# A convolution and SwiGLU kernel: block 0 convolved on TensorE by doubled diagonals, weights cast by GpSimd transfers, another order in the last block

## The chip, the core and the metric

The kernel runs on one NeuronCore of a Trainium2 chip. The metric is device time in microseconds (us), as the median of several executions. One more execution was taken by the hardware profiler; all durations below are from it, and "the profile" and "the trace" mean it. Engine names: PE is TensorE, DVE is VectorE, ACT is ScalarE, POOL is GpSimd, SP is SyncE (here only a DMA queue). An instruction named L320 stands on line 320 of the kernel as it is before the change.

## The reference

```python
w = softmax(weight, axis=-1)              # 8 heads x 7 taps
x_pad = zeros(6 rows) ++ x                # x: 8 x 4096 x 192, causal
conv[b, s, h, :] = sum_k w[h, k] * x_pad[b, s + k, h, :]    # 24 channels a head
y = conv.reshape(32768, 192)
out = (silu(y @ w_gate) * (y @ w_val)) @ w_out              # 192 -> 1536 -> 192
```

A depthwise convolution of seven taps, shared by the 24 channels of a head, feeds a gated feed-forward layer over 32768 tokens. Input and output are float32; the kernel multiplies in float16 and accumulates in float32.

## The kernel before, in words

**Tiling.** Tokens are taken in 64 blocks of 512 (TB). Two blocks are a pair. 192 channels are 128 + 64, so a pair of blocks is laid out as three groups of 128 partitions: group 0 holds channels 0 to 127 of the pair's first block, group 1 the last 64 channels of the first block and the first 64 of the second, group 2 the rest of the second block. Each group is convolved as one tile of 128 x 512 (xc), and a copy with its two halves of 64 partitions exchanged (xs, made by two small transfers on SP, L283 and L284) lets every 64 channels be met from either half of the PE array.

**A block's matmuls.** The 1536 features are 12 chunks of 128. I number the chunks through the run: 0 to 11 are block 0, 12 to 23 block 1, 24 is the first chunk of block 2. For each chunk `first` issues three steps; a step is one matmul for the gate on the lower 64 rows of the array (L313) and one for the value on the upper 64 rows (L314), which run side by side, so that a step takes the time of one. Then `gate` gives ACT a silu (L318) and DVE the product h = silu * val (L320). `second` issues the output matmuls (L325) of the block before, eight to a chunk, into a pair of banks (acc), and after six chunks ACT copies acc out (`evacuate`, L363) and SP stores it (L355). PSUM holds two gate buffers, three value buffers, one buffer for a convolution's running sum (run) and acc, which takes two banks and has one buffer.

**The order around it.** Nothing is scheduled automatically: each engine executes its instructions in the order in which the program issues them. The convolution of a later pair is strewn over the chunks by a plan (PLAN, `at_chunk`, `plan_group`): x is cast into a DRAM copy by a POOL transfer (L80), transposed by a transfer on SP (L85), and for each group, from a chunk c on, ACT makes tap 0 (run, L249) at c and two more taps at c+2 and c+4 (L253), DVE adds two taps at c+1 and c+3 (L260), POOL makes two taps (L267) and adds everything up (L273, L277) from c+4, and SP exchanges the halves at c+11. For pair 1 the three c are 6, 10 and 16. The run buffer is single, so a group's tap 0 waits until DVE has finished the group before it.

**The opening (block 0 and 1 before the plan runs).** x of both blocks is loaded by SP (L105); the softmax of the taps is computed on 8 partitions and spread to all channels by fp32 matmuls (L193, wn_ps). Blocks 0 and 1 are cast by POOL and ACT (L199 to L202), transposed by PE (L228, L230) and convolved as three groups: group 0 by ACT and DVE taps (L249, L253, four DVE taps L260, joined at L277), group 1 on PE by 14 matmuls with diagonal matrices (L390; a weight's float16 part and the rest, seven taps each), group 2 by ACT, DVE and POOL after that, beside block 0's first chunks. Two PE matmuls with a permutation exchange halves (L411). The first four chunks' gate and value weights are staged in float32 by SP (L122) and cast by ACT and POOL (L394, L418); the other weights are cast by POOL's transfers (L127). `warm` issues idle matmuls (L165).

**The end.** After chunk 767, the last block's output matmuls follow in four runs of 12 pairs over four banks (acc, one gate buffer, one value buffer), with two copies and a store after the third and the fourth.

Of the kernel before, what the change touches and what calls it, by code (L numbers as in the profile page):

```python
# [14 lines left out]
    first=(6, 10, 16),  # L15
# [7 lines left out]
def kernel(  # L23
# [68 lines left out]
    def sync_after(ins, earlier, why="one bank, two halves of the array"):  # L92
# [8 lines left out]
    taps = const_pool.tile([H, K], fp32, tag="taps", name="taps")  # L101
    nc.sync.dma_start(out=taps, in_=weight)
    x_sb = xpool.tile([P, 2 * SUBS, D], fp32, tag="x_sb", name="x_sb", bufs=1)
    halves = [
# [4 lines left out]
        for b in range(2)  # L109
    ]  # L110

    C1 = 4 * P
    w = wpool.tile([P, 3, Dff], fp16, tag="w_sb", name="w_sb")
    w_st = wpool.tile([P, 3, C1], fp32, tag="w_st", name="w_st")
# [5 lines left out]
    for rows, src in w_halves:  # L120
        sync_after(
            nc.sync.dma_start(out=w_st[rows, :, :], in_=src[:, :, 0:C1]), halves[0], "x goes first"  # L122
        )

    def load_w(lo, hi, which):
        rows, src = w_halves[which]
        nc.gpsimd.dma_start(out=w[rows, :, lo:hi], in_=src[:, :, lo:hi])  # L127

    ident32 = const_pool.tile([P, P], fp32, tag="ident32", name="ident32")
    make_identity(nc, ident32)  # L130
    ident = const_pool.tile([P, P], fp16, tag="ident", name="ident")
    nc.vector.tensor_copy(ident, ident32)

    swapper = const_pool.tile([P, P], fp16, tag="swapper", name="swapper")
    nc.vector.tensor_copy(swapper[:, 0:DB], ident[:, DB:P])
    nc.vector.tensor_copy(swapper[:, DB:P], ident[:, 0:DB])
# [4 lines left out]

    opening = ctx.enter_context(ExitStack())
    pool0 = opening.enter_context(tc.tile_pool(name="xts0", bufs=1, space=bass.MemoryType.PSUM))


    zeros = const_pool.tile([P, TB], fp16, tag="zeros", name="zeros")
    nc.vector.memset(zeros, 0.0)
    early = {
        n: pool0.tile(shape, dt, tag=n, name=n)
        for n, shape, dt in (  # L150
            ("xt_act", [P, DB + TB], fp16),
            ("wn_ps", [P, 3, K], fp32),
            ("xtB", [P, DB + TB], fp16),
            ("xt", [P, DB + TB], fp16),
            ("sumB", [P, TB], fp32),
            ("swB", [P, TB], fp32),
            ("idle", [P, TB], fp32),
            ("xtC", [P, DB + TB], fp16),
        )
    }  # L160
    idle = early["idle"]

    def warm(n):
        for _ in range(n):
            nc.tensor.matmul(idle, ident, zeros, start=True, stop=True)  # L165


    own = const_pool.tile([H, 2 * D], fp32, tag="own", name="own")
    nc.gpsimd.memset(own, 1.0)
    for m in (own[:, 0:D], own[:, D:]):  # L170
        nc.gpsimd.affine_select(
            out=m, in_=m, pattern=[[1, D]],
            compare_op=ALU.is_ge, fill=0.0, base=0, channel_multiplier=-grp,
        )
        nc.gpsimd.affine_select(
            out=m, in_=m, pattern=[[-1, D]],
            compare_op=ALU.is_ge, fill=0.0, base=grp - 1, channel_multiplier=grp,
        )
    head = {n: const_pool.tile([H, 1], fp32, tag=n, name=n) for n in ("wmax", "wsum", "wrec")}
    soft = const_pool.tile([H, K], fp32, tag="soft", name="soft")  # L180
    warm(4)
    nc.vector.tensor_reduce(head["wmax"], taps, axis=AX.X, op=ALU.max, negate=True)  # L182
    nc.scalar.activation(soft, taps, AF.Exp, bias=head["wmax"])
    nc.scalar.activation(two, one, AF.Silu)
    nc.vector.tensor_reduce(head["wsum"], soft, axis=AX.X, op=ALU.add)
    nc.vector.tensor_scalar(head["wsum"], head["wsum"], scalar1=1e-9, scalar2=None, op0=ALU.add)
    nc.vector.reciprocal(head["wrec"], head["wsum"])
    nc.vector.tensor_scalar(soft, soft, scalar1=head["wrec"], scalar2=None, op0=ALU.mult)

    wn_ps = early["wn_ps"]  # L190
    wn = const_pool.tile([P, 3, K], fp32, tag="wn", name="wn")
    for g in range(3):
        nc.tensor.matmul(wn_ps[:, g, :], own[:, ts(g, P)], soft, start=True, stop=True)  # L193
    warm(2)
    nc.vector.tensor_copy(wn, wn_ps)

    x16 = xpool.tile([P, 1 + SUBS, 2, D], fp16, tag="x16", name="x16", bufs=1)
    nc.gpsimd.memset(x16[:, 0, 0, :], 0.0)
    nc.gpsimd.tensor_copy(x16[:, 1:, 0, 0:P], x_sb[:, 0:SUBS, 0:P])  # L199
    nc.scalar.copy(x16[:, 1:, 0, P:D], x_sb[:, 0:SUBS, P:D])  # L200
    nc.scalar.copy(x16[:, :, 1, 0:DB], x_sb[:, SUBS - 1 :, 0:DB])
    nc.gpsimd.tensor_copy(x16[:, :, 1, DB:D], x_sb[:, SUBS - 1 :, DB:D])  # L202
    for b in range(2):
        load_w(C1, 2 * C1, b)

# [8 lines left out]

    class Group:


        def __init__(self, p, g, pool=cpool):
            self.p, self.g, self.w, self.pool = p, g, wn[:, g, :], pool
            if p:  # L220
                self.xc_in = xts[p][:, g, HIST - pad :]
            self.parts = []

        def rows(self, s):
            return x16[:, s, :, :].rearrange("p b c -> p (b c)")[:, ts(self.g, P)]

        def turn(self, xt, reader=None):
            nc.tensor.transpose(xt[:, 0:DB], self.rows(0)[DB:P, :], ident[DB:P, DB:P])  # L228
            for s in range(SUBS):
                nc.tensor.transpose(xt[:, DB + s * P :][:, 0:P], self.rows(s + 1), ident)  # L230
# [24 lines left out]
        def dve_tap(self, k, psum=False, last=False):  # L255
            v, s = self.tap(k, psum)
            run = self.aD
            if last:
                self.aD = self.pool.tile([P, TB], fp32, tag="aD", name="aD")
# [286 lines left out]
```

## Time and profile before

| what | value |
|---|---|
| median of 3 runs | 780.12 us (780.05, 780.12, 781.20) |
| profiled execution, its own device time | 780.98 us |
| its span from first to last instruction | 779.2 us |
| mean granted PE clock | 0.998 |
| PE busy | 767.4 us, 98% of the span, 10800 matmuls |
| DVE, ACT, POOL busy | 632.8, 661.0, 647.7 us |
| first gate matmul of chunk 0 | 15.47 us |
| first output matmul of block 0 (chunk 12) | 29.03 us |
| last PE matmul begins | 775.5 us |

Start times are counted from the span's start. A timeline row gives start, duration, engine, line, operation, output and input tiles, count, and in brackets how long the engine had idled before and what released it. A busy PE is not a PE at its peak: consecutive matmuls overlap, and what counts is the distance between starts. In the steady part a step of `first` starts every 0.21 us and a pair of output matmuls every 0.08 us.

### The profile page before, as it was taken

The page shows a single profiled execution, that of the slowest core. Times are in us where ns is not written, and L with a number is a line of the kernel's source. Part 1 is how long each engine was busy: PE and PEld are TensorE (multiplying, and loading weights), DVE is VectorE, ACT ScalarE, POOL GpSimd, SP SyncE. Part 2 cuts the span into 40 slices and gives each one's busy share as a digit, 9 for nine tenths or more (in the row PEclk, how much of TensorE's full clock was granted, in tenths as well). Part 3 has the DMA queues.
Part 4 walks back from the last instruction along what each step waited for, and adds up shares of the span by engine and source line. Part 5 has one row for each costly group of instructions (what it writes and reads, how often), then busy time and mean ns, then how long its engine had stood idle before and what let it go on. Part 6 is the DMA issues. An engine that isn't in the chain of part 4 may idle for free.

```text
span 779.2 us, 27410 instructions
## 1 busy us (share of the span) xinstructions
PE 767.4 (98%) x10800; PEld 587.8 (75%) x10800; DVE 632.8 (81%) x980; ACT 661.0 (85%) x1207; POOL 647.7 (83%) x612
## 2 busy tenths in 40 slices
PE   7899999999999999999999999999999999999998
PEld 3567777777777777777777777777777777777776
DVE  6778888888888888888888888888888888888874
ACT  6788888888888888888888888888888888888874
POOL 6799988888888988888988888988888988888820
PEclk9999999999999999999999999999999999999999
DMA  8643553543444454434443435443435443624111
GB/s 154 105 96 67 95 81 89 96 96 68 94 79 93 94 78 86 95 74 98 92 89 77 94 73 99 91 90 77 95 68 102 91 88 81 94 69 103 46 46 53
DMA packets 137186, 67.36 MB, mean 86 GB/s; under 512 B 90080, under 2 KB 136672, under 8 KB 137056
## 3 DMA queue, kind: packets, MB, share of 16 engines
q1 hardware_dynamic: 101440, 51.65, 26.2%
q0 software_dynamic: 35616, 13.95, 16.7%
q8 instruction: 84, 1.38, 0.7%
q14 instruction: 46, 0.38, 0.2%
HBM read 29.47 MB, written 37.74 MB: 86 GB/s over the span
## 4 chain that ended last, share of the span: by engine, by line
PE 97%; ACT 1%; POOL 1%; DMA 0%; DVE 0%; issue 0%; SPq 0%; POOLq 0%; DVEq 0%; ACTq 0%
PE val L314 49%; PE acc L325 34%; PE gate L313 11%; PE sumB L390 1%; ACT silu L318 1%; DMA xs<-xc 0%; PE idle L165 0%; POOL t L273 0%; ACT t L253 0%; DVE h L320 0%; PE wn_ps L193 0%; POOL xc L277 0%; PE gate L325 0%; PE val L325 0%; ACT xc L398 0%
## 5 line engine op out<-in xcount | busy, mean ns | idle before, releaser
L320 DVE TENSOR_TENSOR h<-silu,val 128x512 f16<-128x512 f16 x768 | 512.5, 685 | 133.6 <-ACT silu L318 97.7
L318 ACT ACTIVATE silu<-gate 128x512 f16<-128x512 f32 x768 | 449.3, 593 | 83.2 <-PE gate L313 80.0
L325 PE MATMUL acc<-wo_sb,h 64*128 64x192 f16 x6096 | 474.7, 243 | 0.2 <-DVE h L320 0.2
L325 PEld LDWEIGHTS <-h 64*128 64x128 f16 x6144 | 402.2, 94 | 65.9 <-issue 2.6
L313 PE MATMUL gate<-xs,w_sb 64*128 64x512 f16 x1152 | 428.9, 377 | 1.3 <-ACT silu L318 1.3
L313 PE MATMUL gate<-xc,w_sb 64*128 64x512 f16 x1152 | 428.4, 377 | 1.0 <-ACT silu L318 0.9
L273 POOL TENSOR_TENSOR t<-t,t 128x512 f32<-128x512 f32 x281 | 356.6, 1269 | 85.4 <-ACT t L253 51.6
L314 PE MATMUL val<-xc,w_sb 64*128 64x512 f16 x1152 | 424.0, 377 | 1.1 <-DVE h L320 1.0
L314 PE MATMUL val<-xs,w_sb 64*128 64x512 f16 x1152 | 373.2, 377 | 1.7 <-DMA xs<-xc 1.7
L314 PEld LDWEIGHTS <-w_sb 64*128 64x128 f16 x2304 | 209.4, 94 | 106.9 <-issue 6.0
L313 PEld LDWEIGHTS <-w_sb 64*128 64x128 f16 x2304 | 209.8, 94 | 6.2 <-issue 3.2
L267 POOL TENSOR_SCALAR t<-xt,wn 128x512 f32<-128x512 f16 x186 | 139.0, 828 | 2.2 <-DMA xt<-x16d 2.2
L253 ACT ACTIVATE t<-xt,wn 128x512 f32<-128x512 f16 x186 | 132.6, 713 | 0.0
L277 POOL TENSOR_TENSOR xc<-t,aD 128x512 f16<-128x512 f32 x94 | 119.0, 1266 | 8.0 <-DVE aD L260 0.7
L363 ACT COPY o<-acc 128x384 f32<-128x384 f32 x126 | 60.3, 479 | 20.6 <-PE acc L325 9.1
L260 DVE SCALAR_TENSOR_TENSOR run<-xt,wn,run 128x512 f32<-128x512 f16 x93 | 69.7, 749 | 0.0
L260 DVE SCALAR_TENSOR_TENSOR aD<-xt,wn,run 128x512 f32<-128x512 f16 x93 | 69.0, 742 | 0.0
L249 ACT ACTIVATE run<-xt,wn 128x512 f32<-128x512 f16 x93 | 63.8, 686 | 1.1 <-DVE aD L260 1.1
L80 POOL DMA_DIRECT2D x16d<-in_x_dram x31 | 39.1, 1261 | 0.0
L165 PE MATMUL idle<-zeros,ident 128*128 128x512 f16 x6 | 2.9, 620 | 2.6 <-DVE wmax L182 2.6
L390 PE MATMUL sumB<-xcin,diag 128*128 128x512 f16 x14 | 5.1, 525 | 0.0
L260 DVE SCALAR_TENSOR_TENSOR aD<-xcin,wn,aD 128x512 f32<-128x512 f16 x4 | 3.9, 971 | 0.1
(73 smaller groups left out, 51.3 us busy)
## 6 DMA issues: line engine op xcount, KB each, us to landing
out_dram<-o SPq DMA_DIRECT2D x128, 192.0 KB, 2.2
x16d<-in_x_dram POOLq DMA_DIRECT2D x31, 396.0 KB, 6.1
xs<-xc SPq DMA_DIRECT2D x188, 64.0 KB, 2.8
x_sb<-in_x_dram SPq DMA_DIRECT2D x2, 384.0 KB, 3.6
wo_sb<-in_moe_w_out_dram POOLq DMA_DIRECT2D x1, 576.0 KB, 8.3
xt<-x16d SPq DMA_TRANSPOSE x31, 4.0
w_st<-in_moe_w_gate_dram SPq DMA_DIRECT2D x1, 384.0 KB, 4.4
w_st<-in_moe_w_val_dram SPq DMA_DIRECT2D x1, 384.0 KB, 5.3
```

Source lines behind the costliest of these rows:

```text
L249: nc.scalar.mul(self.aD, *self.tap(0, psum, xt))
L253: nc.scalar.mul(self.parts[-1], *self.tap(k, psum, xt))
L260: nc.vector.scalar_tensor_tensor(out=self.aD, in0=v, scalar=s, in1=run, op0=ALU.mult, op1=ALU.add)
L267: nc.gpsimd.tensor_scalar(self.parts[-1], v, scalar1=s, scalar2=1.0, op0=ALU.mult, op1=ALU.mult)
L273: nc.gpsimd.tensor_tensor(self.parts[0], self.parts[0], t, op=ALU.add)
L277: (eng or nc.gpsimd).tensor_tensor(xc, self.parts[0], self.aD, op=ALU.add)
L313: nc.tensor.matmul(g, w[0:DB, ca, f], a[0:DB, :], start=(i == 0), stop=(i == 2))
L314: nc.tensor.matmul(v, w[DB:P, cb, f], b[DB:P, :], start=(i == 0), stop=(i == 2))
L318: nc.scalar.activation(s, self.g.pop(j), AF.Silu)
L320: nc.vector.tensor_tensor(h, s, self.v.pop(j), op=ALU.mult)
L325: ins = nc.tensor.matmul(acc, self.h[j][r, ts(s, P)], wo_r[r, j, :], start=first and j == 0, stop=not first and j == NCH - 1, skip_group_c ...
L363: nc.scalar.copy(self.o[:, 2 * half : 2 * half + 2, :], self.acc[:, :, 0:D])
```

## The change

Loads: SP loads x first, the taps come on ACT's queue, and all gate and value weights come by six POOL transfers of four chunks and one half of the array each, which cast on the way. The float32 staging tile and its two casts are gone.

Taps: the softmax is no longer divided on 8 partitions. Exponentials and their sum are spread together, and each channel is divided afterwards (`normalize`), first for the two layouts that block 0 needs, and for the two that later groups need at the end of the opening.

Block 0 is convolved wholly on PE. Channels 0 to 127 (A) are multiplied by diagonals that stand doubled, so that each half of 64 channels comes out on both halves of the partitions, in two banks (sum0, sum1), for the float16 part (`hi`) and for the rest (`lo`). The last 64 channels (C) are stored twice, so that one matmul of 128 rows takes both parts (`sum2`). No half of block 0 has to be exchanged any more. Block 1's channels A are convolved by ACT, DVE and POOL taps in the opening, its channels C on PE during chunks 0 to 4 (`lateC`).

Pair 1 of the plan starts at chunks 5, 9 and 16, with three DVE taps and one POOL tap to a group. Chunks 0 and 1 issue their first two steps before either's third.

The end: in the last block the copy out of acc is issued behind the chunk's silu, and the last runs of output matmuls leave chunk 11's pieces for later.

```diff
-    first=(6, 10, 16),
+    first=(5, 9, 16),
...
-    for rows, src in w_halves:
-        sync_after(nc.sync.dma_start(out=w_st[rows, :, :], in_=src[:, :, 0:C1]), halves[0], "x goes first")
+    load_w(0, 4, 0)
+    load_w(0, 4, 1)
...
+            ("xtA", [P, TB], fp16), ("xtC", [P, TB], fp16), ("sum0", [P, TB], fp32),
+            ("sum1", [P, TB], fp32), ("wn_ps", [P, 4, K + 1], fp32), ("sum2", [P, TB], fp32),
+            ("xtA1", [P, DB + TB], fp16),
...
+    def normalize(lo, hi):
+        nc.vector.reciprocal(wrec[:, lo:hi], wn_ps[:, lo:hi, K])
+        nc.vector.tensor_tensor(
+            wn[:, lo:hi, :], wn_ps[:, lo:hi, 0:K],
+            wrec[:, lo:hi].unsqueeze(2).to_broadcast([P, hi - lo, K]), op=ALU.mult,
+        )
+    warm(5)
...
+    spread(0, 2)
+    warm(3)
+    normalize(0, 2)
+    cast_a(nc.gpsimd.tensor_copy, 0, 2)
+    cast_a(nc.scalar.copy, 2, 4)
+    cast_c(nc.vector.tensor_copy, 0, 4)
+    load_w(4, 8, 0)
+    cast_a(nc.gpsimd.tensor_copy, 4, 8)
+    load_w(4, 8, 1)
+    turn(early["xtA"], colA, 0, False)
+    turn(early["xtC"], colC, 0, False)
+    warm(1)
+    nc.vector.tensor_copy(hi, wn[:, 0, :])
+    diagonal(dg["hi"], hi, 0, 4)
+    nc.scalar.copy(xcA[:, pad:], early["xtA"])
+    for k in range(4, K):
+        nc.scalar.mul(dg["hi"][:, k, :], twin, wn[:, 0, k : k + 1])
...
+    diagonal(dg["lo"], lo, 0, K)
+    def conv_a(d, first):
+        for k in range(K):
+            for r, bank in ((slice(0, DB), "sum0"), (slice(DB, P), "sum1")):
+                nc.tensor.matmul(early[bank], d[r, k, :], xcA[r, k : k + TB], ...)
+    def conv_c(bank, xc):
+        for k in range(K):
+            nc.tensor.matmul(bank, dg["C"][:, k, :], xc[:, k : k + TB], ...)
+    conv_a(dg["hi"], True)
+    turn(early["xtA1"], colA, SUBS, True)
+    spread(2, 4)
+    conv_a(dg["lo"], False)
+    for k in range(K):
+        nc.scalar.mul(dg["C"][:, k, :], twin, partC32[:, k : k + 1])
+    nc.scalar.copy(xcC[:, pad:], early["xtC"])
+    conv_c(early["sum2"], xcC)
+    emit_cast(1)
+    cast_c(nc.gpsimd.tensor_copy, 4, 8)
+    for b in range(2):
+        load_w(8, NCH, b)
...
+    nc.vector.tensor_scalar(sumA1, v, scalar1=s, scalar2=None, op0=ALU.mult)
+    dveA1(1)
+    nc.scalar.mul(actA1[0], *tapA1(5))
+    nc.scalar.copy(D0, early["sum0"])
+    nc.vector.tensor_copy(D1, early["sum1"])
+    nc.scalar.mul(actA1[1], *tapA1(6))
+    nc.scalar.copy(D2, early["sum2"])
+    for k in (2, 3, 4):
+        dveA1(k)
+    nc.gpsimd.tensor_tensor(actA1[0], actA1[0], actA1[1], op=ALU.add)
+    nc.gpsimd.tensor_tensor(xA1, actA1[0], sumA1, op=ALU.add)
+    nc.gpsimd.dma_start(out=wo_r, in_=moe_w_out.rearrange("(c p) d -> p c d", p=P))
+    normalize(2, 4)
...
-            for k, o in zip(dves, PLAN["taps"]):
+            for k, o in zip(dves, PLAN["taps"] if q > 1 else (1, 2, 3)):
...
+    def lateC(step):
+        if step == 0:
+            late["xt"] = tpool.tile([P, DB + TB], fp16, tag="run", name="run")
+            turn(late["xt"], colC, SUBS, True)
+        elif step == 1:
+            nc.scalar.copy(xcC1, late["xt"][:, DB - pad :])
+        elif step == 2:
+            late["sum"] = apool.tile([P, 2, 512], fp32, tag="acc", name="acc")
+            conv_c(late["sum"][:, 0, :], xcC1)
+        else:
+            nc.scalar.copy(D2b, late["sum"][:, 0, :])
+    for step, c in enumerate((0, 1, 2, 4)):
+        at_chunk(c, lambda step=step: lateC(step))
...
+                if block.n == 0 and j < 2:
+                    if j == 0:
+                        block.first(0, (0, 1))
+                        block.first(1, (0, 1))
+                    block.first(j, (2,))
                 if end:
-                    before.evacuate(j // 6)
+                    if block.n < 2 * n_pairs - 1:
+                        before.evacuate(j // 6)
                     block.first(j)
                 block.gate(j)
+                if end and block.n == 2 * n_pairs - 1:
+                    before.evacuate(j // 6)
...
-    for lo, hi, first in ((0, 1, True), (2, 3, True), (1, 0, False), (3, 2, False)):
-        for j in range(NCH):
-            before.piece("lo", lo, j, banks[lo], first)
-            before.piece("hi", hi, j, banks[hi], first)
-        if (lo, hi) == (1, 0):
-            nc.scalar.copy(before.o[:, 0:2, :], acc[:, :, 0:D])
-            before.store(0)
+    run(0, 1, range(NCH - 1), True)
+    run(2, 3, range(NCH - 1), True)
+    run(0, 1, (NCH - 1,), True)
+    run(2, 3, (NCH - 1,), True)
+    run(1, 0, range(NCH), False)
+    nc.scalar.copy(before.o[:, 0:2, :], acc[:, :, 0:D])
+    before.store(0)
+    run(3, 2, range(NCH), False)
```

The built program of the changed kernel, whose order of instructions and waits can be read without running it, shows two waits that the source does not spell out. The value buffer of chunk 1 lies in the bank of wn_ps, so chunk 1's first value matmul waits for the second `normalize`. And ACT and DVE never read the bank of xtA1 at the same time: ACT's tap 5 waits for DVE's tap 1, and DVE's taps 2 to 4 wait for ACT's tap 6.

## The prediction

> **What bounds the kernel now.** I read the profile page's chain first: PE carries 97% of it. So the question is where PE is not working at its pace, and for that I cut the span into stages (the table of busy time by window: start:end, length, then busy us of PE, PEld, DVE, ACT, POOL, and at the end the granted clock, the DMA share and GB/s).
>
> ```profile
> 15.46:24.00 8.54, 6.80 (x43) 2.61 (x43) 6.94 (x9) 5.02 (x9) 4.28 (x4) 0.80 1.38 194
> 24.00:36.00 12.00, 10.39 (x119) 6.08 (x117) 10.09 (x16) 10.27 (x20) 9.03 (x9) 1.00 0.45 69
> 36.00:46.00 10.00, 8.28 (x117) 5.72 (x115) 7.63 (x13) 7.78 (x15) 9.58 (x9) 1.00 0.61 108
> 46.00:60.00 14.00, 14.00 (x203) 10.81 (x199) 11.03 (x18) 12.02 (x23) 13.36 (x13) 1.00 0.31 79
> ```
>
> From 46 us on PE has no gap until 770. Before that it lacks 1.74 + 1.61 + 1.72 = 5.1 us, and 15.47 us pass before the first gate matmul. The change touches only this beginning and the last block, so everything is decided in chunks 0 to 23 and 756 to 767. PE's own timeline says where the gaps are:
>
> ```profile
> 15.47 0.39 PE L313 MATMUL gate<-xc,w_sb 64*128 64x512 f16 x1
> 17.92 0.37 PE L313 MATMUL gate<-xc,w_sb 64*128 64x512 f16 x1 [0.70 <-ACT silu L318]
> 19.99 0.58 PE L314 MATMUL val<-xc,w_sb 64*128 64x512 f16 x1 [1.04 <-DVE h L320]
> 31.03 0.37 PE L313 MATMUL gate<-xs,w_sb 64*128 64x512 f16 x1 [1.32 <-ACT silu L318]
> 41.82 0.38 PE L313 MATMUL gate<-xc,w_sb 64*128 64x512 f16 x1
> 44.35 0.37 PE L314 MATMUL val<-xs,w_sb 64*128 64x512 f16 x1 [1.72 <-DMA xs<-xc]
> ```
>
> Chunk 24 starts at 41.82 and loses 1.72 to a late exchange; it stands as if it had started at 43.54. That is **my mark**: after it nothing differs until chunk 756.
>
> The third row shows the clock: matmuls of 0.58 to 0.63 us instead of 0.38, starting every 0.43 instead of 0.21. The windows around it:
>
> ```profile
> 9.68:13.09 3.41, 3.41 (x13) 1.38 (x12) 3.20 (x5) 1.16 (x3) 3.01 (x4) 1.00 0.62 102
> 16.51:19.92 3.41, 1.74 (x14) 0.51 (x11) 3.34 (x5) 2.44 (x5) 1.75 (x2) 1.00 1.38 187
> 19.92:23.33 3.41, 3.34 (x16) 1.36 (x17) 2.25 (x5) 1.19 (x2) 2.05 (x2) 0.50 1.39 194
> ```
>
> After 3.41 us with PE half busy (1.74) the clock is halved for 3.41 us. At the start it is slow too, though the clock column, which knows only changes, says 1.00: the first seven L390 matmuls start every 0.43 us, and full pace comes near 13.1, after a window nearly all of large matmuls. The two windows before it, with 57% large matmuls (1.45 + 0.5 of 3.41) and with mostly transposes, did not bring it.
>
> The Trainium skill (TensorE: Matmul & The Clock Gate, Part 1) has a free-running window of about 3.4 us and halves the clock after an idle window. The length agrees with 3.41. That PE must idle a whole window doesn't: here two gaps of 0.70 and 1.04 and some drain were enough. By the skill's words no gap below would cost a clock, and the time would be 781.4 after an early clock and 783.9 after a late one.
>
> **The opening up to the diagonals.** Ends of rows before, reused: POOL has the identity at 1.37 and one mask (memset, two selects of 0.34) at 2.4. ACT issues the taps' load (0.41) ahead of a table load of 1.28, so its Exp runs 2.7 to 3.0; two DVE rows of 0.15 and 0.14 follow, 3.4. Two fp32 spreads cost 0.48 each (1.44 for three): 4.4. Three idle matmuls at 0.43: 5.7. The casts are ready by then: x lands 3.3 us after its issue, now at 0.8 instead of 1.27, so at 4.1; POOL, after two transfers (1.5) and small copies, casts by 5.1; DVE's cast of C (0.6, between 0.41 and 1.08) ends at 5.5. Four transposes take 0.6, ACT's copy to xcA 0.58: the diagonals start at **7.1** (8.88 before). DVE's `hi` (0.30) and four diagonals (0.65, from 1.08 for seven) are ready at 6.5.
>
> **PE's convolution.** It grows from 14 slots to 21 (7 hi, 7 lo, 7 C; the two halves of A run side by side), with five transposes (0.6) and two spreads (0.96) between hi and lo. At 0.43 a slot lo ends at 7.1 + 3.0 + 1.5 + 3.0 = **14.6**. If the full clock comes early in hi, at about 9.0, 4.5 slots at 0.43 and 2.5 at 0.215 end at 9.55, the middle costs 1.0, lo 1.5: **12.05**. The windows that can bring it are 72 to 88% large matmuls, where I know 57% as too little and about 80% as enough: even odds.
>
> **The new wait.** Chunk 1's first value matmul waits for `normalize(2, 4)`, at the end of a chain that begins with lo's last matmul: 0.22 until ACT sees it (14.28 to 14.52 before L398), copy D0 0.48 to the next start, tap 6 0.67, then on DVE three taps from PSUM at 0.78 (3.11 for four at 9.03) and two rows of 0.15 to 0.2: 0.22 + 0.48 + 0.67 + 2.35 + 0.45 = **4.2 us**. Queued behind the waiting matmul are all later chunks. Beside the wait PE has conv C (1.5 to 3.0) and two and a half steps (0.5 to 1.0), so 0.3 to 2.2 us of it are bare. Chunk 1 resumes at R = 18.8 or 16.25.
>
> **From R to the mark,** each engine in order, with distances between starts from rows: silu 0.48, ACT tap 0.61, h 0.60, DVE tap 0.66, step 0.21, POOL sum 1.27. First silu R+0.8; `lateC` puts its copy (0.5) behind the second silu and conv C (1.5) before chunk 3, which starts at R+4.1. ACT's D2b copy and tap 0 of group 0 then delay silu 6 to R+7.6, and from h 6 (R+8.2) DVE is full: three taps lie between products 6 and 9, so the third ends at R+12.1. ACT's tap 0 of group 1 waits for it, and behind that stand tap 2 (0.61) and silu 10, R+13.35, on which chunk 12's gate buffer depends: chunk 12 starts at R+14.0, 1.9 after PE was free. This is the 31.03 gap of before, grown by a third tap. Block 1 takes 12 x 0.976 and about 0.6 of waits for h: chunk 24 at **R + 26.35**. POOL's chain per group loses a tap and a sum, 0.68 + 1.27: group 1 ends at R+20.6 and its exchange, behind a store, lands at about R+25.4, so the 1.72 goes. Sum: 45.15 (+1.6 on the mark) or 42.6 (-0.9). In the second case PE idles 2.2 us before R, which in the trace's manner loses the clock: half of 3.41, +1.7, so 44.3 (+0.8).
>
> **Costed at nothing:** the weight transfers (issued by 3.9, 5.4 us to land, needed after 14), x16d (landing before 15, its turn before 22, needed at R+7), w_out (landing at 28, needed at R+14). Their cover is the same R; if it shrank by 5 us, w_out would bind.
>
> **The last block.** Rows of ACT and PE:
>
> ```profile
> 770.73 0.48 ACT L363 COPY o<-acc 128x384 f32<-128x384 f32 x1 [0.26 <-PE acc L325]
> 771.18 0.60 ACT L318 ACTIVATE silu<-gate 128x512 f16<-128x512 f32 x1
> 771.25 1.08 PE L325 MATMUL acc<-wo_sb,h 64*128 64x192 f16 x22
> 772.55 0.26 PE L325 MATMUL acc<-wo_sb,h 64*128 64x192 f16 x2 [0.21 <-DVE h L320]
> ```
>
> The copy uses time in which the silu's gate isn't ready (its last matmul ends at 771.14), so putting the silu first gains 0.04. But the copy then starts at 771.64, ends at 772.12, and PE's next acc pieces start at 772.16 instead of 771.25: +0.9. The same at chunk 761: 765.76 becomes 766.31, +0.55. Leaving chunk 11's pieces for later saves PE's wait for h, 772.15 to 772.55: -0.4. The third run now follows its own bank's mark (a nop on SP) after two pairs; no row shows that wait, between 0 and 0.5, I take 0.25. Together **+1.3**.
>
> **Sum,** against the profiled 780.98 (span 779.2 and 1.8 around it; it lies 0.86 above the median): late clock 780.98 + 1.6 + 1.3 = 783.9; early clock, lost in the wait, 780.98 + 0.8 + 1.3 = 783.1. I forecast **783.5**, own range 782.2 to 784.9 (hand errors of about 1).
>
> **Rivals.**
> - Early clock, kept through the wait: -0.9 + 1.3, 781.4. For it: windows can split the gap. Against: 1.74 of 3.41 lost it. 18%. (It is what the Trainium skill's section named above would give.)
> - Late clock and lost as well: 1.6 + 1.7 + 1.3, 785.6. For it: with conv C partly fast, PE idles about 2 us before R. 13%.
> - Faster: early clock kept, and silu 10 not held behind the third tap (DVE catches up before product 6, from R+8.2 on about 2 us earlier), so -0.9 - 1.9; the copies of the last block find ACT idle early enough and only the 0.4 counts: 777.8. It decides if h 6 comes before R+6.3. Against it: ACT's five extra rows lie before it. 13%.
> - That the change doesn't do what it says: the staging casts were off the path before (chunk 0 needs only L394's 0.51 at 10.78), so "all weights by GpSimd" is worth nothing; this is inside every case.
>
> Forecast 56%. A measurement tells 0.2% (1.56 us) from no change: faster 13%, within 18%, slower 69%. The range leaves out most of the faster case and the end of the slowest: 779.5 to 786.2.
>
> **What would show it.** Diagonals' first matmul near 7.1; lo's last at 12 to 14.6; chunk 1's first value matmul 4.2 us after that, released by DVE `normalize`; chunk 12 about 14 us after it, released by a silu behind ACT's run; no wait on xs at chunk 24; in the last block two PE gaps of 0.6 and 0.9 released by ACT's copy. The prediction is wrong if PE goes on to chunk 1 without waiting for DVE, if DVE's taps of pair 1 don't hold ACT, or if the copies of the last block don't hold PE.

## The result and the profile after

The changed kernel takes 781.84 us in the median of 20 executions, the kernel before 780.28: the ratio is 1.0023, 95% interval [1.0016, 1.0030]. It is slower, as forecast, but by 1.56 us and not by 3.2 (783.5 against that median). The profiled execution took 781.48, span 779.8, which is 0.50 above the profiled 780.98 of before. Four of the 20 executions have a mean clock of 0.998 and lie between 783.37 and 783.87; the others have 1.0 and lie between 781.11 and 782.22. (One window of 3.413 us at half clock is 0.002 of the span.)

First PE's timeline, as before: start, duration, line, tiles, and in brackets the idle time and what ended it.

```profile
7.23 2.31 PE L277 MATMUL sum<-xcA,dghi 64*128 64x512 f16 x14
...
10.37 1.69 PE L277 MATMUL sum<-xcA,dglo 64*128 64x512 f16 x14
...
13.61 0.39 PE L396 MATMUL gate<-D,w_sb 64*128 64x512 f16 x1
...
16.02 0.39 PE L397 MATMUL val<-D,w_sb 64*128 64x512 f16 x1 [1.59 <-DVE wn L216]
...
18.69 1.67 PE L284 MATMUL acc<-xcC,dgC 128*128 128x512 f16 x7 [0.52 <-ACT xcC L533]
...
27.75 0.37 PE L397 MATMUL val<-D,w_sb 64*128 64x512 f16 x1 [0.43 <-DVE h L403]
...
30.26 0.39 PE L396 MATMUL gate<-xA,w_sb 64*128 64x512 f16 x1 [1.70 <-ACT silu L401]
...
42.66 0.39 PE L396 MATMUL gate<-xc,w_sb 64*128 64x512 f16 x1
```

`hi` takes 2.31 us where seven slots at half clock would be 3.0: the full clock comes inside it. The fourth row is the new wait for `normalize`. The last row is chunk 24, without a wait for xs: 42.66, where the mark of before was 43.54. Against that profile the opening gains 0.88. But that profile had lost the clock once (the window from 19.92 in the prediction), which most executions of the kernel before do not: of 75 timed beside the experiments, 58 have a mean clock of 0.999 or 1.0 and a median of 780.27, and 17 have 0.997 or 0.998 and lie between 780.58 and 782.40.

The same time by windows of 3.413 us, counted on from 8.54, where the trace's record of the clock has its change to full (columns as in the prediction):

```profile
11.95:15.36 3.41, 2.48 (x14) 0.81 (x12) 2.62 (x4) 1.96 (x4) 1.27 (x1) 1.00 1.02 144
15.36:18.77 3.41, 2.23 (x19) 1.03 (x20) 1.84 (x5) 1.81 (x4) 2.94 (x3) 1.00 0.67 142
...
25.60:29.01 3.41, 2.44 (x17) 0.70 (x12) 3.35 (x6) 1.62 (x3) 1.27 (x1) 1.00 0.39 50
29.01:32.43 3.42, 2.17 (x30) 1.37 (x32) 2.19 (x4) 3.12 (x7) 2.49 (x2) 1.00 0.39 81
```

The granted clock stays 1.00: the boundaries at 15.36 and 29.01 cut both long gaps in two, and no window has PE busy for less than 2.17. Last, the two rows of PE at the end:

```profile
765.43 0.51 PE L408 MATMUL acc<-wo_sb,h 64*128 64x192 f16 x8 [0.40 <-ACT o L446]
...
771.86 1.08 PE L408 MATMUL acc<-wo_sb,h 64*128 64x192 f16 x22 [1.03 <-ACT o L446]
```

Both gaps end with ACT's copy. To price the end I take the copy at chunk 755, the last that stands alike in both kernels, and the last copy of all, first before the change and then after it:

```profile
759.00 0.48 ACT L363 COPY o<-acc 128x384 f32<-128x384 f32 x1 [0.26 <-PE acc L325]
...
775.84 0.32 ACT L515 COPY o<-gate 128x192 f32<-128x192 f32 x1 [0.54 <-PE gate L325]
```

```profile
757.91 0.48 ACT L446 COPY o<-acc 128x384 f32<-128x384 f32 x1
...
776.31 0.32 ACT L608 COPY o<-gate 128x192 f32<-128x192 f32 x1 [0.54 <-PE gate L408]
```

From the one to the other it is 16.84 us before and 18.40 after: the end loses 1.56. At the first copy the changed kernel is 1.09 ahead; 1.56 - 1.09 = 0.47, about the difference of the profiles.

### The profile page after: what moved, and what is told of

It reads as the page before. It is cut to its first block, busy times and chain, and to the rows that moved or that the text cites. A ratio compares the mean times of both kernels' runs of the same rounds, so it can differ in the third digit from the quotient of the medians.

```text
span 779.8 us, 27470 instructions
## 1 busy us (share of the span) xinstructions
PE 768.6 (99%) x10829; PEld 504.6 (65%) x10829; DVE 632.0 (81%) x985; ACT 660.0 (85%) x1213; POOL 640.9 (82%) x609
## 4 chain that ended last, share of the span: by engine, by line
PE 97%; ACT 1%; DVE 1%; issue 1%; ACTq 0%; DVEq 0%
PE gate L396 59%; PE acc L408 32%; PE val L397 4%; PE sum L177 1%; ACT silu L401 0%; DVE sumA L462 0%; PE sum L277 0%; PE acc L284 0%; PE val L408 0%; ACT t L330 0%; PE wn_ps L212 0%; ACT o L446 0%; DVE aD L344 0%; PE gate L408 0%; PE xtA L243 0%
## 5 line engine op out<-in xcount | busy, mean ns | idle before, releaser
L357 POOL TENSOR_TENSOR t<-t,t 128x512 f32<-128x512 f32 x276 | 349.8, 1267 | 91.5 <-ACT t L330 57.3
L396 PE MATMUL gate<-xs,w_sb 64*128 64x512 f16 x1128 | 419.6, 376 | 0.0
L396 PE MATMUL gate<-xc,w_sb 64*128 64x512 f16 x1116 | 415.0, 376 | 0.0
L397 PE MATMUL val<-xc,w_sb 64*128 64x512 f16 x1116 | 410.3, 376 | 0.0
L408 PEld LDWEIGHTS <-h 64*128 64x128 f16 x6144 | 283.8, 94 | 140.4 <-issue 2.0
L397 PE MATMUL val<-xs,w_sb 64*128 64x512 f16 x1128 | 364.9, 376 | 0.0
L408 PE MATMUL acc<-wo_sb,h 64*128 64x192 f16 x6096 | 361.5, 243 | 1.5 <-ACT o L446 1.4
L396 PEld LDWEIGHTS <-w_sb 64*128 64x128 f16 x2304 | 209.0, 94 | 116.1 <-ACT silu L401 4.0
L397 PEld LDWEIGHTS <-w_sb 64*128 64x128 f16 x2304 | 203.9, 94 | 5.5 <-DVE wn L216 2.1
L397 PE MATMUL val<-D,w_sb 64*128 64x512 f16 x36 | 9.4, 378 | 2.0 <-DVE wn L216 1.6
L396 PE MATMUL gate<-D,w_sb 64*128 64x512 f16 x36 | 9.4, 377 | 0.5 <-ACT silu L401 0.3
```

The costliest lines, as they stand in the source:

```text
L357: nc.gpsimd.tensor_tensor(self.parts[0], self.parts[0], t, op=ALU.add)
L396: nc.tensor.matmul(g, w[0:DB, ca, f], a[0:DB, :], start=(i == 0), stop=(i == 2))
L397: nc.tensor.matmul(v, w[DB:P, cb, f], b[DB:P, :], start=(i == 0), stop=(i == 2))
L408: ins = nc.tensor.matmul(acc, self.h[j][r, ts(s, P)], wo_r[r, j, :], start=first and j == 0, stop=not first and j == NCH - 1, skip_group_c ...
```

## The experiments

My theory after the trace: the opening gains about 1 us when the clock comes early and stays; of its gain the wait for `normalize` and the gap at chunk 12 take back a good part; the end loses 1.3 to 1.6. Rivals: the gaps are only places where another bound shows, and the 783.6 of four executions comes from something else than chunk 12. Medians below are set against the kernel before as timed beside each (780.26 to 780.49); the changed kernel stands at +1.56.

### The end: copies first in the new kernel, new end in the old

```diff
-                    if block.n < 2 * n_pairs - 1:
-                        before.evacuate(j // 6)
+                    before.evacuate(j // 6)
                     block.first(j)
...
-                if end and block.n == 2 * n_pairs - 1:
-                    before.evacuate(j // 6)
```

> The changed kernel, with the copies of the last block's chunks 5 and 11 put back ahead of the silu. The changed kernel lies 1.56 us above the one before. Theory (the copies behind the silu hold PE's next acc pieces, two gaps of 0.40 and 1.03): the first gap goes, of the second some 0.1 stays, so 1.3 to 1.4 us less than the changed kernel, 0.1 to 0.3 above the one before; the opening unchanged, chunk 24 at 42.7. Rival (PE would have waited there anyway, for h or for the mark on SP): the gap moves to the next wait, and the time stays within 0.4 us of the changed kernel.

780.0 against 780.49, ratio 1.0000 [0.9989, 1.0011]. From the copy at chunk 755 to the last it is 16.71 us (760.16 to 776.87), 1.69 less than in the changed kernel. The theory holds for the two gaps, but by the medians the edit is worth 2.05 and not 1.3 to 1.4. Some of that is the comparison: beside it the kernel before lost its clock in 11 of 31 executions, and among executions with a clock of 0.999 or more the edit is worth 1.8. Its profile fell on a lost clock:

```profile
30.97 0.60 PE L396 MATMUL gate<-xA,w_sb 64*128 64x512 f16 x1 [1.71 <-ACT silu L401]
```

```profile
27.06:30.47 3.41, 1.75 (x12) 0.52 (x10) 2.61 (x5) 1.62 (x4) 0.63 (x1) 1.00 0.64 109
30.47:33.89 3.42, 2.92 (x20) 1.47 (x22) 2.94 (x5) 2.14 (x4) 3.20 (x3) 0.50 0.05 10
```

Here the full clock began at 9.99, and the gaps in chunk 11 and before chunk 12 (0.43 and 1.70) lie in one window: PE busy 1.75 of 3.41, then half clock. In the changed kernel's own profile the same gaps lay on both sides of a boundary.

The other way round, the old kernel with the new end alone:

```diff
                 if end:
-                    before.evacuate(j // 6)
+                    if block.n < 2 * n_pairs - 1:
+                        before.evacuate(j // 6)
                     block.first(j)
                 block.gate(j)
+                if end and block.n == 2 * n_pairs - 1:
+                    before.evacuate(j // 6)
...
-    for lo, hi, first in ((0, 1, True), (2, 3, True), (1, 0, False), (3, 2, False)):
+    for lo, hi, js, first in (
+        (0, 1, range(NCH - 1), True), (2, 3, range(NCH - 1), True),
+        (0, 1, (NCH - 1,), True), (2, 3, (NCH - 1,), True),
+        (1, 0, range(NCH), False), (3, 2, range(NCH), False),
+    ):
```

> The kernel before, with the changed kernel's last block alone: copies behind the silu in its chunks 5 and 11, and chunk 11's pieces behind the other runs' eleven. Theory: two gaps of 0.4 and 1.0 on PE behind ACT's copy, the wait for h of 0.4 gone, 0.25 of a wait for SP's mark: 1.2 to 1.6 us more than the kernel before, 781.5 to 781.9. Rival (the loss in the changed kernel's tail depends on its opening, through another phase of the last block): less than 0.5 us more.

781.75 against 780.31, ratio 1.0017 [1.0009, 1.0026], and 18.21 us for the stretch of 16.84. The theory holds: 1.44 more, where 1.2 to 1.6 was expected, and the end costs nearly the same with either opening. As copies first alone give 16.71, the other order of chunk 11's pieces gains 0.13.

This run also weighs the two openings against each other, with the same end behind both: 781.75 with the old one, 781.84 with the new one (781.71 and 781.66 in executions with a clock of 0.999 or more). So the new opening gains nothing that can be measured, and of the change's 1.56 all but some 0.1 is its end. The trace of this run has the old opening without a lost clock:

```profile
758.41 0.48 ACT L363 COPY o<-acc 128x384 f32<-128x384 f32 x1 [0.26 <-PE acc L325]
```

Against it the changed kernel's profile is 0.50 ahead at this copy, not 1.09; and that profile, at 781.48, is one of the faster executions of its kernel.

### The new wait: wn_ps in a bank of its own

```diff
-            ("wn_ps", [P, 4, K + 1], fp32),
+            ("spare", [P, TB], fp32),
             ("sum2", [P, TB], fp32),
             ("xtA1", [P, DB + TB], fp16),
+            ("wn_ps", [P, 4, K + 1], fp32),
```

> The changed kernel, with wn_ps in an eighth PSUM bank and its old bank left empty, so that chunk 1's first value matmul no longer waits for the normalization. Theory of the prediction (everything up to the mark is counted from that wait's end): PE's gap of 1.6 us at 14.4 goes, chunk 3 starts at about 18.5 instead of 20.29, chunk 24 at about 40.9 instead of 42.66: 1.5 to 1.8 us less than the changed kernel. Rival (the path runs through the convolution of pair 1, whose begin is bound to chunk 5 and whose exchange to POOL and SP): PE starts chunk 1 sooner, but gets the time back as a wait for silu, h or xs before 43 us; less than 0.5 us gained.

780.37 against 780.49, ratio 0.9997 [0.9988, 1.0006]: 1.7 less than the changed kernel. PE's wait before chunk 1 is gone, chunk 24 starts at 41.09, and the gap at chunk 12 stays 1.70 (28.69 instead of 30.26). The theory holds: what is won before R (chunk 1's first value matmul) arrives whole at the mark (1.57, although the full clock came at 9.39 here and at 8.54 in the changed kernel). The gap at chunk 12 lies in a window with PE busy 1.71, and the next one still has the full clock:

```profile
26.46:29.87 3.41, 1.71 (x21) 0.77 (x19) 2.13 (x4) 3.04 (x6) 1.49 (x2) 1.00 0.41 68
29.87:33.28 3.41, 3.31 (x45) 2.05 (x43) 3.41 (x7) 2.64 (x5) 3.25 (x4) 1.00 0.29 67
```

### What stands ahead of that wait: the low part left out

```diff
-    diagonal(dg["lo"], lo, 0, K)
...
-    conv_a(dg["lo"], False)
```

> The changed kernel without the second half of block 0's convolution of its first 128 channels: the fourteen matmuls with the low part of the fp16 weights and the DVE instruction that makes their diagonals are left out. Theory (PE's slots up to the last of them stand one for one ahead of the chain that ends in the normalization): chunk 1's first value matmul comes 1.3 to 1.6 us sooner, and chunk 24 and the end with it, 780.3 to 780.6. Rival (the DVE taps of block 1's part, which begin at 9.9 whatever the matmuls do, set the normalization): less than 0.5 us sooner.

783.30 against 780.31, ratio 1.0043 [1.0031, 1.0055]. Seven slots less, and 1.4 us more than the changed kernel, which neither theory nor rival had. Chunk 1's first value matmul came at 15.95, as in the changed kernel (16.02). PE waited elsewhere:

```profile
11.67 1.68 PE L283 MATMUL sum<-xcC,dgC 128*128 128x512 f16 x7 [1.79 <-ACT xcC L292]
...
15.95 0.39 PE L395 MATMUL val<-D,w_sb 64*128 64x512 f16 x1 [1.86 <-DVE wn L216]
```

ACT's seven products for conv C, which need DVE's `partC`, began at 9.00 here and at 7.85 in the changed kernel, mainly because a DVE cast of seven elements a partition took 1.05 beside POOL instead of 0.16. From there copies and tap 6 run to 13.25, and DVE's last three taps wait for them. A second chain thus took the place of the first, and what the seven slots cost where DVE isn't late stays open. What the profile does show is that PE, idle in two stretches, loses the clock, at 17.64 (after a window with 1.69 busy) and again at 31.29 (1.35). The second loss belongs to the gaps around chunk 12, which the changed kernel has too; all six executions have a mean clock of 0.998 or less.

### The gap at chunk 12

In the changed kernel ACT stands still before its first product of group 1, until DVE's third tap of group 0 has ended, and the silu for which chunk 12 waits stands behind that product:

```profile
28.39 0.69 ACT L334 ACTIVATE run<-xt,wn 128x512 f32<-128x512 f16 x1 [1.79 <-DVE aD L344]
```

Two taps on DVE and two on POOL:

```diff
-        npl = PLAN["npool"] if q > 1 else 1
+        npl = PLAN["npool"]
...
-            for k, o in zip(dves, PLAN["taps"] if q > 1 else (1, 2, 3)):
+            for k, o in zip(dves, PLAN["taps"]):
```

> The changed kernel, with pair 1 planned as all other pairs are: two taps on DVE and two on POOL instead of three and one. Theory (the third DVE tap holds ACT's first product of group 1, and with it silu 10 and chunk 12): the gap of 1.70 at chunk 12 falls to 0.5 to 0.9, but POOL's chain is longer by a tap and a sum a group (1.95 us), so group 1's exchange lands 1 to 2 us later and the wait for xs at chunk 24 comes back with 1.5 to 2 us: in all 0.3 to 1.0 us more than the changed kernel. Rival (POOL has time to spare, since it is idle for 5.6 us from 20 on): no wait at chunk 24, and 0.8 to 1.2 us less than the changed kernel.

782.11 against 780.49, ratio 1.0019 [1.0010, 1.0027], the same as the changed kernel within 0.1. Chunk 12 came 13.58 us after R instead of 14.24, so the third tap costs its own 0.66 and no more; PE's gap (1.65) hardly shrank because PE arrived sooner (the gap of 0.43 in chunk 11 is gone). And the wait for xs came back with 1.18. So the rival falls, and of the theory only the returning wait came true.

ACT not held, with the running sum in SBUF:

```diff
-            self.aD = tpool.tile([P, TB], fp32, tag="run", name="run")
+            pool = const_pool if (self.p, self.g) == (1, 1) else tpool
+            self.aD = pool.tile([P, TB], fp32, tag="run", name="run")
```

> The changed kernel, with the running sum of group 1 of pair 1 in a buffer of its own in SBUF, so that ACT's first product of group 1 needn't wait until DVE's third tap of group 0 has freed the one PSUM buffer. Theory (PE's 1.70 at chunk 12 is ACT, in order, standing 1.79 us before that product, with a product and silu 10 behind it): ACT no longer waits there, chunk 12's first gate matmul comes at about 12.5 us after chunk 1's first value matmul instead of 14.2; DVE, with a product and a tap a chunk at 1.26 us, then gives part of it back as waits for h in chunks 12 to 16; chunk 24 is 0.8 to 1.2 us earlier, and so is the end. Rival (DVE is the bound, ACT's wait only shows it): waits for h of the same sum, less than 0.3 us gained.

781.68 against 780.26, ratio 1.0016 [1.0007, 1.0024]; chunk 24 at R + 26.59 (changed kernel 26.64). ACT's wait is gone and chunk 12 starts at 28.62, but nothing is left of it at chunk 24. DVE's timeline from chunk 9 on:

```profile
28.53 1.28 DVE L404 TENSOR_TENSOR h<-silu,val 128x512 f16<-128x512 f16 x2
29.72 1.66 DVE L345 SCALAR_TENSOR_TENSOR run<-xt,wn,run 128x512 f32<-128x512 f16 x1
31.30 0.67 DVE L404 TENSOR_TENSOR h<-silu,val 128x512 f16<-128x512 f16 x1
31.90 0.74 DVE L345 SCALAR_TENSOR_TENSOR run<-xt,wn,run 128x512 f32<-128x512 f16 x1
32.56 0.67 DVE L404 TENSOR_TENSOR h<-silu,val 128x512 f16<-128x512 f16 x1
33.16 1.16 DVE L345 SCALAR_TENSOR_TENSOR aD<-xt,wn,run 128x512 f32<-128x512 f16 x1
```

DVE has no idle time, and two of the three taps take 1.66 and 1.16 instead of 0.75, both begun while POOL was at a sum: 1.3 us lost. (The tap at 31.90 began ahead of POOL's sum at 32.02 and kept its 0.74; that sum took 1.74 instead of 1.27.) So the rival holds for this kernel, but the experiment brought a cost of its own: with the sum in PSUM the taps stay at 0.75. The Trainium skill (SBUF — State Buffer, Who interferes with whom) says that a DVE instruction with two SBUF inputs contends with a POOL instruction that reads SBUF; the rows agree. What a second PSUM buffer would gain wasn't tried.

Pair 1 begun sooner:

```diff
-    first=(5, 9, 16),
+    first=(3, 7, 16),
```

> The changed kernel, with pair 1's groups begun at chunks 3 and 7 instead of 5 and 9 (the third stays at 16). Theory (from 19 to 21 us ACT and DVE are idle while PE convolves the last part of block 1, and what stands between chunk 3 and the mark is that pair 1's convolution starts too late): group 0's first product moves from 23.2 to about 22, the gap of 1.70 at chunk 12 falls below 0.5, no wait for xs at chunk 24, which starts at about 41.0 to 41.5: 1.2 to 1.7 us less than the changed kernel. Rival (ACT and DVE are full from chunk 3 on whatever the order): the products then delay silus 4 to 8, PE's gaps move to chunks 5 to 9, and the time stays within 0.4 us.

782.54 against 780.49, ratio 1.0023 [1.0013, 1.0032], 0.5 more than the changed kernel. The gap did not shrink, it moved with group 1's start, from chunk 12 to chunk 10, and there it lay in one window (1.56 busy) and cost the clock:

```profile
28.32 0.53 PE L396 MATMUL gate<-D,w_sb 64*128 64x512 f16 x1 [1.70 <-ACT silu L401]
```

Chunk 24 came at R + 27.60; by my estimate it would be 25.9 without the half of 3.41, so that 0.7 was gained and 1.7 lost. But the lost clock isn't all: two of the nine executions have a mean clock of 1.0 and took 782.65 and 782.69, and what they lost isn't shown. The theory fails: group 1's first product waits for group 0's last tap here too (1.37 us of ACT). The rival, with gaps in chunks 5 to 9 and within 0.4 us, misses narrowly.

The new plan in the old kernel:

```diff
-    first=(6, 10, 16),
+    first=(5, 9, 16),
...
+        npl = PLAN["npool"] if q > 1 else 1
...
+            for k, o in zip(dves, PLAN["taps"] if q > 1 else (1, 2, 3)):
```

> The kernel before, with the changed kernel's plan for pair 1 alone: groups begun at chunks 5, 9 and 16, three taps on DVE and one on POOL. Theory of the prediction (the plan takes away the wait of 1.72 for the exchange at chunk 24, and costs up to 0.66 at chunk 12 for DVE's third tap): no wait at chunk 24, 0.9 to 1.5 us less than the kernel before. Rival (with three taps DVE is full for six chunks, and the wait only moves from the exchange to h): within 0.3 us of the kernel before.

782.70 against 780.31, ratio 1.0033 [1.0022, 1.0045]. Both theories fail. All six executions have a mean clock of 0.996 to 0.998; the profile, which is of the slowest (784.57), lost it from 20.07, as the kernel before did from 19.92, and from 47.37, after a window with PE busy 1.48. The wait for xs stays:

```profile
46.30 0.37 PE L314 MATMUL val<-xs,w_sb 64*128 64x512 f16 x1 [1.94 <-DMA xs<-xc]
```

POOL was done with group 1 at 38.1, but SP issued the exchange only at 40.83 (in SP's order it stands behind the nop that waits for output matmuls of chunk 20), and it landed late (all transfers of xs in that stretch):

```profile
L283 SPq DMA_DIRECT2D xs<-xc x1: 467/467/467, 40.8 to 40.8; - x1
L284 SPq DMA_DIRECT2D xs<-xc x1: 588/588/588, 41.3 to 41.3; - x1
...
DMA to landing us min/median/max: 4.9/5.1/5.3
```

In the kernel before it is POOL that releases the exchange, and this is what the prediction had seen:

```profile
38.72 1.27 POOL L277 TENSOR_TENSOR xc<-t,aD 128x512 f16<-128x512 f32 x1
...
40.02 0.46 SPq L283 DMA_DIRECT2D xs<-xc  x1
```

In the changed kernel POOL is done at 37.19, the same pair is issued at 39.95, and it landed in 2.6 to 2.9 us. The fetch of pair 2's rows (x16d, 396 KB, 7.7 us to landing) is issued 2.8 us ahead of the exchange in both, at 38.02 here and at 37.13 there, so it doesn't tell the two landings apart; what made this one late isn't shown.

### The clock

Four idle matmuls in the gap ahead of chunk 12, on top of the copies first:

```diff
+    def fill():
+        for _ in range(4):
+            nc.tensor.matmul(late["sum"][:, 1, :], zeros[:, 0:P], zeros, start=True, stop=True)
+
+    at_chunk(11, fill)
```

> The changed kernel, with the last block's copies ahead of the silu (as in the first experiment, 780.0 with four of eleven runs near 782) and four idle matmuls of 0.21 each put into PE's gap ahead of chunk 12, in a PSUM half that is unused then. Theory of the clock (windows of 3.413 us at a phase that differs from run to run; a window with PE busy for half of it or less is followed by one at half clock; the window that holds the gaps before chunks 11 and 12 falls under half at some phases only): with 0.85 us more of PE's work in that window it never falls under half, so that none of the runs lies near 782 and all have a mean clock of 0.999 or 1.0; the median is 779.5 to 780.0. Rival (the runs near 782 come from elsewhere, a late transfer or a late clock at the start): three to five of eleven stay there.

779.90 against 780.26, ratio 0.9996 [0.9987, 1.0005]. The slowest of eleven executions took 780.55; of the eleven without the fill four lay between 781.75 and 782.73. Chunk 12 came at R + 14.23, as in the changed kernel. This is as the theory has it, and against the rival, which expected three to five executions near 782. The evidence is a count: without the fill 8 of 31 executions (eleven with the copies first and twenty of the changed kernel) lost the clock, and at that rate eleven in a row without a loss would come about four times in a hundred. The profile fell on a phase at which nothing is lost without the fill either.

Without the nine idle matmuls of the opening:

```diff
-    warm(5)
...
-    warm(3)
...
-    warm(1)
```

> The changed kernel without its nine idle matmuls (five at the start, three after the first spread, one ahead of the diagonals). Theory (the full clock begins at the first window boundary after a window that is mostly large matmuls; in the five profiles of this opening it began between 7.9 and 10.0 us because the idle matmuls filled the windows ahead of the diagonals): it now begins 1 to 3 us later, between 9.5 and 13, chunk 1's first value matmul moves from 15.7 to 16.7 up to 17 to 18.8, and the kernel takes 1 to 2.5 us more than the changed one. Rival (the diagonals themselves bring the clock within a window, since they are dense from 7.2 on): the same phases as before, and within 0.4 us of the changed kernel.

783.93 against 780.26, ratio 1.0047 [1.0033, 1.0061]; all five executions lie between 783.32 and 784.95. The price is as expected, the way to it in the profile is another: the full clock came at 9.81, not later, R was 16.14, and the half clock came from 30.29 on, after a window with 1.35 busy that holds the gaps around chunk 12. Why four of five executions lost it here, and four of twenty in the changed kernel, isn't shown. One execution has a mean clock of 1.0 and took 783.98, so there is a second way, perhaps the late clock; no profile shows it.

### The pieces together

Copies first, the bank of its own and the running sum in SBUF, in one kernel:

```diff
+                    before.evacuate(j // 6)
...
+            ("wn_ps", [P, 4, K + 1], fp32),
...
+            pool = const_pool if (self.p, self.g) == (1, 1) else tpool
```

> The changed kernel with three edits together: the last block's copies ahead of the silu, wn_ps in its own PSUM bank, group 1's running sum of pair 1 in SBUF. Theory (three separate places on the path, whose gains add): 1.4 to 2.0 from the copies, 1.6 from the bank, 0.8 to 1.2 from the sum, together 3.8 to 4.8 us less than the changed kernel, 777.2 to 778.2, which is 2.3 to 3.3 below the kernel before. Rival (the opening's two places share one bound, pair 1's convolution and its exchange through POOL and SP): a wait for xs at chunk 24 takes back the second gain; 778.5 to 779.

777.71 against 780.26, ratio 0.9968 [0.9955, 0.9980]: 4.1 below the changed kernel and 2.5 below the one before. Chunk 24 starts at 40.60, no window from the full clock to 46 us has PE busy under 2.4. The gains add to within 0.3: alone the three edits won 2.05, 1.7 and 0.1 of the changed kernel's time. The rival falls; no wait for xs came back.

On top of it, pair 1's rows fetched sooner:

```diff
-    first=(5, 9, 16),
+    first=(2, 6, 16),
...
+    emit_cast(1)
     load_w(4, 8, 0)
...
-    if n_pairs > 1:
-        emit_cast(1)
     cast_c(nc.gpsimd.tensor_copy, 4, 8)
```

> The kernel with three edits (777.7), and pair 1's rows fetched sooner: its transfer is issued on GpSimd ahead of the second pair of weight transfers instead of behind them (at 4.8 instead of 6.9 us), and its groups begin at chunks 2 and 6 instead of 5 and 9. Theory (what stands between chunk 3 and the mark is DVE, which from chunk 6 to 16 has a product and a tap a chunk, while it is idle for 1.9 us beside the convolution of block 1's last part): the transposed rows land at about 18 instead of 20.3, DVE's taps begin in chunk 3, and chunk 24 starts at about 39.0 instead of 40.6: 1.6 us less, 776.1. Rival (PE's own pace from chunk 12 on, or the order on ACT, is the bound): the gaps move to chunks 4 to 9, at most 0.5 us gained, and with them a half clock of 1.7 us in some runs.

778.25 against 780.31, ratio 0.9983 [0.9969, 0.9997]; seven executions between 777.28 and 778.29, five between 779.89 and 782.02. The profile (778.29) shows a loss that neither theory had listed: `hi` starts at 8.93 instead of 7.22, for want of its diagonals. DVE's rows:

```profile
6.09 1.37 DVE L264 CAST hi<-wn 128x7 f16<-128x7 f32 x1
7.50 1.38 DVE L258 TENSOR_TENSOR dghi<-twin,hi 128x512 f16<-128x512 f16 x1
```

The cast of seven elements took 0.19 in the changed kernel. Here POOL, shifted by the transfer, casts x beside it (6.29 to 7.15). Chunk 0 starts 1.12 later than without this edit (14.69 against 13.57), chunk 24 only 0.57 (41.17 against 40.60): pair 1's chain gained about 0.5, as the rival has it, and the opening took it back twice over. What the five slower executions lost isn't shown; their mean clocks of 0.999 and 1.0 speak against the rival's half clock.

## Why the prediction was right in sign and wrong in size

- **The opening up to R** was right for the early clock: diagonals 7.23 (forecast 7.1), `lo` over at about 11.86 (12.05; seven slots from 10.37), R 16.02 (16.25), 4.16 us after that (4.2).
- **The clock is the step that failed.** I gave "even odds" to the full clock coming early in `hi`, and said that the wait before R "in the trace's manner loses the clock". Ten profiles with these idle matmuls have the full clock between 7.26 and 9.99; the late case is in none of them. (Executions without a profile can't be told apart, as the recorded clock knows only changes.) And the wait before R, priced at 2.2 us of idle, is 1.59. Eight losses in fourteen profiles followed windows with PE busy 1.74, 1.75, 1.56, 1.35, 1.69, 1.35, 1.69 and 1.48 us of 3.413; the lowest windows that lost nothing had 1.71, 1.77, 1.78, 1.82 and 1.82. The limit is half of the window to within some 0.05, and 1.59 of idle leaves 1.82 busy at the worst phase, so by these figures it doesn't lose the clock. With the clock early and kept, my 18% rival came (781.4; the profile took 781.48), and against that profile the forecast was 2.0 too high, 1.7 of it for a clock that was not lost.
- **The phase of the window** moves R as well: in six profiles with R in this form it goes from 15.72, with the full clock at 7.93, to 16.74, with 9.99. That is about as wide as the 781.11 to 782.22 of the executions with a clock of 1.0; that it is their cause is my reading.
- **The sign came from the end alone.** I had the opening at +0.8 to +1.6. It is -0.88 against the profile of before and nothing in the medians, since that profile, the base of my sum, had itself lost the clock. I had seen that it lay 0.86 above the median and not asked why. So "slower" was right by the last block's term, and the opening's term had the wrong sign.
- **Where the clock is at risk** I had not priced: the gaps of 0.43 in chunk 11 and 1.70 before chunk 12 together exceed half a window, and are in one or cut in two by the phase. That fits the four executions of twenty near 783.6, though none of them was profiled.
- **From R to the mark** was right in time: chunk 3 at R + 4.27 (4.1), silu 6 at R + 7.84 (7.6), the third tap's end at R + 12.33 (12.1), chunk 12 at R + 14.24 (14.0), chunk 24 at R + 26.64 (26.35). Less so in cause: "this is the 31.03 gap of before, grown by a third tap" holds for 0.66 of it. The rest looks like DVE, which from chunk 6 on has a product and a tap for each chunk: with ACT freed, PE waited for h instead. But there DVE's taps had also become longer, so this is argued and not shown.
- **The wait for xs** went, as forecast, and the longer chain on POOL brought it back (1.18). But the shorter chain alone was not enough: the old kernel with it kept the wait. Once POOL is done sooner, the exchange stands behind the mark at chunk 20; it landed at about R + 27 and not at R + 25.4, just when PE, itself late from chunk 12, came to it (42.9). That there was no wait was a near thing, as landings varied from 1.9 to 5.3 us between kernels.
- **The last block** was forecast at +1.3 and measured +1.56 in the profiles and +1.44 in the old kernel's medians: the copies cost 1.69 (0.9 + 0.55 forecast), the order gained 0.13 (-0.4 + 0.25). This term carries the whole result.
- **The faster case** (777.8) needed h 6 before R + 6.3; DVE's h 6 began at 24.50, R + 8.5. It was rightly small.

The Trainium skill (TensorE: Matmul & The Clock Gate, Part 1) has the free-running window of 3413 ns: the runs agree, all changes of the clock lie whole multiples of 3.413 apart (9.99 and 30.47 in the first experiment are six). It has half clock "after ≥1 idle window"; the runs do not agree, a window with PE busy for half of it was enough. By the skill's rule no gap here costs a clock, which gives the 781.4 of the profile but leaves the four executions near 783.6 unexplained.

## What to carry to other kernels

Before a profile becomes the base of a sum, ask whether its execution lost a clock: this one had, and it made the new opening look about 0.6 us better than it is at chunk 755. Ask of each gap on PE not how long it is but how much PE does in the worst 3.413 us around it: below half, PE lost another 1.7 us behind the gap in some executions, and with four idle matmuls that only filled waiting time none of eleven did. A buffer that lies in another tile's bank carries that tile's last reader into its first write; one free bank was worth 1.7 us here. And a copy moved behind the work it seemed to delay must be asked who needs its source free.

## What the runs showed of the hardware that was not expected

- The clock's limit at half a window, above, and that a kernel with less PE work can take longer (the one without the low part, 1.4 us, with two windows lost in its profile).
- Short DVE rows beside POOL's casts and transfers grew up to sevenfold: the cast of seven elements a partition from 0.19 to 1.37 us, another from 0.16 to 1.05. A tap with both tensors in SBUF went from 0.75 to 1.66 when it began during a POOL sum, while with one in PSUM it stayed at 0.75.
- An exchange of 2 x 64 KB took between 1.9 and 5.3 us to land.
